# Queuing the conversions of the expert weights behind named pieces of the work under way

## The chip, the cores and the metric

One core of one Trainium2 chip runs the program. The metric is the device time of one execution in microseconds (us); a time shown for a kernel is the median of several executions. The engines are TensorE (PE, with its weight loads as PEld), VectorE (DVE), ScalarE (ACT), GpSimd (POOL) and SyncE (SP, which issues most of the DMAs). Each engine works through its own queue in order: an instruction that waits holds up everything behind it on that engine.

## The reference

Three stages follow each other; the change touches the last one and its seam with the second.

```python
attn_out = _attn_ref(q, k, v, omega)            # linear attention with random features, 4 x 8 heads x 576 x 64
x = attn_out.transpose(0, 2, 1, 3).reshape(2304, 512)
h = x @ w_in                                    # dense: 512 -> 2048
x = np.maximum(0.01 * h, h) @ w_out             # 2048 -> 512
logits = x @ w_gate                             # experts: 8, 512 -> 1024 -> 512
e_idx = np.argmax(logits, axis=1)
...
for e in range(8):
    mask = e_idx == e
    h = np.maximum(x[mask] @ w1[e], 0.0)
    out[mask] = gate_w[mask, None] * eom[mask, e, None] * (h @ w2[e])
```

## The kernel before

Every float32 product is made from two rounded parts: an operand is split into a high and a low part (`hi_lo`: ACT or DVE copies the rounded value, then DVE subtracts it from the source), and TensorE multiplies high by high, high by low and low by high. So each weight has to be converted before it can be used.

**Dense stage.** The 2304 rows go in 9 chunks c of 256 rows, the 2048 inner features in 8 units u. `h_unit(c, u)` is 24 matmuls (L463 to L465) into `hp`, followed on ACT by the copy `g` (L468) and on DVE by the leaky maximum (L469), `gh` and `gl`. `x_unit(c, u)` is 12 matmuls (L482 to L484) that read `gh` and `gl`. The loop issues `h_unit` of the next pair, then `x_unit` of the present one, so TensorE works one unit ahead. The attention of later rows and the routing of finished chunks are woven in by `tick`; the routing ends in two scatters of 4-byte row numbers into the table `tab_d` (L594).

**Expert stage.** The rows of one expert are worked through in slots of 576 rows, NSLOT + 1 = 4 of them in the written-out part (s = 0 to 3). A slot is two blocks (256 rows, then 320 rows). A block first runs `hidden(f)` for f = 0 to 7: 12 matmuls each (L713 to L715) into one of two PSUM banks of `ps_a`, then on ACT the relu `ehh` (L716) and on DVE `ehl` (L717), which free the bank. Then `back(j)` runs for 2 or 3 row tiles: 24 matmuls each (L730 to L732), an eviction `eyr` and a scatter of rows to the output. Before the first two `back` of a block, `xt` transposes the rows of the block that follows and splits them into `exh` and `exl`.

**Weights of an expert.** A slot has 8 weight pieces of 512 KB. `Slot.weight(k)` does all of it in one call: it takes one of two raw buffers `eraw` (tag `wraw`), issues the load on SP (L668 or L670), takes two tiles of a ring of 32, and converts: `ewh` on ACT (L209), `ewl` on DVE (L212). The first slot's pieces are called after the units of the last dense chunk (c = 8, piece u after unit u). The pieces of the slot after the present one are called in both blocks of the present slot after `hidden(f)` for f = 4 to 7, with the number `4 * half + f - 4`.

A list scheduler orders the instructions of each engine ahead of time: by program position, with the instructions that are ready in its own model taken first, so that an instruction called late may be queued early. `high_priority` moves the `g`, `gh`, `gl` of `h_unit` forward. `tc.issue_after(ins)` adds an edge that only fixes order in a queue: what is traced inside it on the engine of `ins` is queued behind `ins`.

Of the kernel before, what the change touches and what calls it, by code (L numbers as in the profile page):

```python
# [16 lines left out]
ALU = mybir.AluOpType  # L17
# [65 lines left out]
def f32(ap):  # L83
    return ap.bitcast(F32)
# [3 lines left out]
def tile_kernel(ctx: ExitStack, tc: tile.TileContext, kT, k_nat, v_nat, qT, q_nat, om, w_in, w_out, wg, w1, w2, out, stop=None, dbg=None):  # L88
# [46 lines left out]
    with ExitStack() as pa:  # L135
# [71 lines left out]
        def hi_lo(dst_hi, dst_lo, src, hi_eng, lo_eng):  # L207
            if hi_eng is nc.scalar:
                nc.scalar.copy(dst_hi, src)  # L209
            else:  # L210
                hi_eng.tensor_copy(dst_hi, src)
            lo_eng.tensor_sub(dst_lo, src, f32(dst_hi))  # L212


        order = [(k, u, h) for u in range(NU) for k in ("in", "out") for h in range(2)]
# [4 lines left out]
        groups = {}  # L220
        both_done = [False]
        newest = []
        kvs = {}
        xdone, hdone = {}, {}
        xT = {}
# [228 lines left out]
        def h_unit(c, u):  # L454
            assert xdone.get(c) == CH * NH // 2, (c, u, xdone)
            hdone[c] = u + 1
            xh, xl = xT[c]
            hp = ps_h.tile([P, 2, CH], F32, name="hp", tag="h")
            wh, wl = win[u]
            for i in range(2):  # L460
                for d in range(ND):
                    a, b_ = wh[:, d, i * P:(i + 1) * P], wl[:, d, i * P:(i + 1) * P]
                    nc.tensor.matmul(hp[:, i, :], a, xh[:, d, :], start=d == 0, stop=False)  # L463
                    nc.tensor.matmul(hp[:, i, :], a, xl[:, d, :], start=False, stop=False)  # L464
                    nc.tensor.matmul(hp[:, i, :], b_, xh[:, d, :], start=False, stop=d == ND - 1)  # L465
            with tc.high_priority(offset=AHEAD):
                g = sb.tile([P, 2, CH], F32, name="g", tag="g", bufs=1)
                nc.scalar.copy(g, hp)  # L468
                nc.vector.scalar_tensor_tensor(g, hp, 0.01, g, op0=ALU.mult, op1=ALU.max)  # L469
                gh = sb.tile([P, 2, CH], F32R, name="gh", tag="gh")  # L470
                gl = sb.tile([P, 2, CH], F32R, name="gl", tag="gl")
                hi_lo(gh, gl, g, nc.vector if c > 1 else nc.scalar, nc.vector)
            return gh, gl

        def x_unit(c, u, gg, acc):
# [173 lines left out]
        class Slot:  # L649


            def __init__(self, num, exp, at, first=False):
                self.c = nc.values_load(num[0:1, ds(at, 1)], engines=[SP], min_val=0, max_val=NC - 1)
                self.e = nc.values_load(exp[0:1, ds(at, 1)], engines=[SP], min_val=0, max_val=NE - 1)
                self.first = first
                self.w = []
                pool = rt if first else eb
                self.idx = pool.tile([P, 5], I32, name="idx", tag="idx", bufs=1 if first else 3)
                whole = tabv[ds(self.c, 1), 0:4 * P].rearrange("o (p i) -> (o p) i", i=4)
                rest = tabv[ds(self.c, 1), 4 * P:SLOT].rearrange("o (p i) -> (o p) i", i=1)  # L660
                for dst, src in ((self.idx[:, 0:4], whole), (self.idx[0:SLOT - 4 * P, 4:5], rest)):
                    got = nc.sync.dma_start(dst, src)
                    behind(got.ins, [o for k, o in placed if k == placed[-1][0]], "the table whole")

            def weight(self, k):
                raw = wst.tile([P, 1024], F32, name="eraw", tag="wraw")
                if k < 4:
                    nc.sync.dma_start(raw, w1v[ds(self.e, 1), k].rearrange("o p f -> (o p) f"))  # L668
                else:
                    nc.sync.dma_start(raw.rearrange("p (i n) -> p i n", i=2), w2v[ds(self.e, 1), k - 4].rearrange("o p i n -> (o p) i n"))  # L670
                hi = wring.tile([P, 1024], F32R, name="ewh", tag="w")
                lo = wring.tile([P, 1024], F32R, name="ewl", tag="w")
                hi_lo(hi, lo, raw, nc.scalar, nc.vector)
                self.w.append((hi, lo))

        class Block:
            def __init__(self, slot, half):
# [27 lines left out]
            def hidden(self, f):  # L705
                if f == 0:
                    self.hh = eb.tile([P, EFF // P, PART], F32R, name="ehh", tag="ehh", bufs=1)
                    self.hl = eb.tile([P, EFF // P, PART], F32R, name="ehl", tag="ehl", bufs=1)
                n = self.n
                t = ps_a.tile([P, 512], F32, name="eht", tag="a")[:, 0:n]  # L710
                for d in range(ND):
                    wh, wl = (w[:, f * P:(f + 1) * P] for w in self.slot.w[d])
                    nc.tensor.matmul(t, wh, self.xh[:, d, 0:n], start=d == 0, stop=False)  # L713
                    nc.tensor.matmul(t, wh, self.xl[:, d, 0:n], start=False, stop=False)  # L714
                    nc.tensor.matmul(t, wl, self.xh[:, d, 0:n], start=False, stop=d == ND - 1)  # L715
                nc.scalar.activation(self.hh[:, f, 0:n], t, AF.Relu)  # L716
                nc.vector.scalar_tensor_tensor(self.hl[:, f, 0:n], t, 0.0, f32(self.hh[:, f, 0:n]), op0=ALU.max, op1=ALU.subtract)  # L717

            def back(self, j, apart=True, final=False):

# [43 lines left out]
        def early():  # L764

            full = counts(ends, "full")
            incl = rt.tile([P, NC], F32, name="incl0", tag="incl0")
            nc.vector.tensor_tensor_scan(incl, ones_f, full, 0.0, op0=ALU.mult, op1=ALU.add)
            nc.vector.scalar_tensor_tensor(picked, incl, 1.0, full, op0=ALU.is_equal, op1=ALU.mult)
            none = rt.tile([P, NC], F32, name="none", tag="none")  # L770
            at = rt.tile([P, 1], F32, name="at", tag="at")
            nc.vector.tensor_scalar(none, incl, 0.0, None, op0=ALU.is_equal, op1=ALU.add, accum_out=at)
            num = rt.tile([1, 1], I32, name="num0", tag="num0")
            nc.vector.tensor_scalar_min(num, at[0:1], NC - 1.0)
            return Slot(num, expert_of(num, 1, "exp0"), 0, first=True)
# [32 lines left out]
        for i, (c, u) in enumerate(pairs):  # L808
# [35 lines left out]
                    tick()  # L844
            if slot is None and c == NCH - 2 and not routes and not any(c_ < 0 for c_, _ in flow):
                slot = early()
            if c == NCH - 1:
                slot.weight(u)
                if u == NU - 2:
                    for d in range(ND):  # L850
                        block.xt(d)
# [21 lines left out]
    with ExitStack() as pb:  # L873
        eb = pb.enter_context(tc.tile_pool(name="eb", bufs=2, reuse_waits="tile"))
        late = [f for it in routes for f in it if f is not nop]
        for s in range(NSLOT + 1):
            for half in range(2):
                last = s == NSLOT and half == 1
                for f in range(EFF // P):
                    block.hidden(f)  # L880
                    if late:
                        late.pop(0)()
                        if not late:
                            num, exp, nsl = listed()
                    if f == 3 and half == 0 and s < NSLOT:
                        other = Slot(num, exp, s)
                    if f >= 4 and s < NSLOT:
                        other.weight(4 * half + f - 4)
                    if f == 3 and not last:
                        following = second if s == half == 0 else Block(slot, 1) if half == 0 else Block(other, 0)  # L890
                        if following is not second:
                            following.rows()
                for j in range(len(block.tiles)):
                    if not last and j < 2:
                        following.xt(2 * j)
                        following.xt(2 * j + 1)
                    block.back(j, final=last)
                block = None if last else following
            slot = other if s < NSLOT else None

        n_slots = nc.values_load(nsl[0:1, 0:1], min_val=NSLOT, max_val=NSLOT + NE)  # L901
        with tc.For_i(NSLOT, n_slots) as s:
            one = Slot(num, exp, s)
            for k in range(8):
                one.weight(k)
            for half in range(2):
                b_ = Block(one, half)
                b_.rows()
                for d in range(ND):
                    b_.xt(d)  # L910
                for f in range(EFF // P):
                    b_.hidden(f)
                for j in range(len(b_.tiles)):
                    b_.back(j, False)
# [69 lines left out]
```

## Time and profile before

| | |
|---|---|
| median of 3 runs | 886.59 us (882.37 to 889.65) |
| profiled execution, its own time | 887.9 us |
| its span, first to last instruction | 886.2 us |
| mean granted TensorE clock | 0.981 of 2.4 GHz |
| busy: PE / PEld / DVE / ACT / POOL | 840.5 / 734.0 / 449.8 / 307.0 / 179.5 us |
| bytes moved by DMA | 73.55 MB, mean 83 GB/s |

The profiled execution is 1.7 us longer than its span. Busy time of TensorE counts overlapping matmuls once. An idle stretch carries the instruction that ended it ("<-"), found from semaphore events.

### The profile page before, as it was taken

How to read it: one execution, taken by the hardware profiler on the slowest of the kernel's cores; microseconds unless marked ns; L12 is line 12 of the kernel's file. 1: busy time of each engine (PE TensorE's matmuls, PEld its weight loads, DVE VectorE, ACT ScalarE, POOL GpSimd, SP SyncE). 2: the span in 40 equal slices, each digit the busy share in tenths (PEclk: the TensorE clock that was granted, in tenths of full speed). 3: DMA queues.
4: the chain of work that ended last, by engine and by line, in shares of the span. 5: the costliest groups of instructions: out<-in, count | busy, mean ns of one | idle time of the engine just before them, and what ended most of it. 6: DMA issues, size and time to landing. Idle time of an engine off the chain costs nothing. (4 is left out here: it accounts for less than half of the span.)

```text
span 886.2 us, 13999 instructions
## 1 busy us (share of the span) xinstructions
PE 840.5 (95%) x5299; PEld 734.0 (83%) x5299; DVE 449.8 (51%) x1142; ACT 307.0 (35%) x755; POOL 179.5 (20%) x253
## 2 busy tenths in 40 slices
PE   9889998999999999999999999997996999999996
PEld 7768777798899899988889899876886779888894
DVE  6899879626545445445554444454335433512220
ACT  4666655424324224323322232142125432411210
POOL 3545544301221012122010010120013211220001
PEclk9899999999999999999999999999999999999998
DMA  7636554301542021152020000155026622410001
GB/s 225 209 116 192 189 179 138 123 1 31 74 108 78 2 43 53 35 97 60 19 43 6 1 25 1 36 186 72 1 94 208 204 80 98 150 54 21 10 24 33
DMA packets 46153, 73.55 MB, mean 83 GB/s; under 512 B 6017, under 2 KB 28673, under 8 KB 46082
## 3 DMA queue, kind: packets, MB, share of 16 engines
q1 hardware_dynamic: 42562, 63.14, 25.7%
q0 software_dynamic: 3520, 9.47, 3.4%
q8 instruction: 44, 0.72, 0.4%
q14 instruction: 27, 0.22, 0.1%
HBM read 62.00 MB, written 10.59 MB: 82 GB/s over the span
## 5 line engine op out<-in xcount | busy, mean ns | idle before, releaser
L463 PE MATMUL hp<-xh,wih 128*128 128x256 f32 x576 | 167.2, 290 | 2.3 <-DVE xl L212 2.0
L464 PE MATMUL hp<-xl,wih 128*128 128x256 f32 x576 | 162.7, 282 | 0.1
L465 PE MATMUL hp<-xh,wil 128*128 128x256 f32 x576 | 162.1, 281 | 0.0
L482 PE MATMUL acc<-woh,gh 128*128 128x512 f32 x288 | 123.8, 430 | 1.4 <-ACT kv L373 1.4
L484 PE MATMUL acc<-woh,gl 128*128 128x512 f32 x288 | 116.6, 406 | 6.8 <-DVE gl L212 6.8
L319 ACT ACTIVATE h<-pw,bias 128x128 f32<-128x128 f32 x288 | 84.8, 372 | 107.5 <-DVE bias L311 87.7
L469 DVE SCALAR_TENSOR_TENSOR g<-hp,g 128x512 f32<-128x512 f32 x72 | 49.6, 689 | 130.7 <-ACT g L468 118.8
L483 PE MATMUL acc<-wol,gh 128*128 128x512 f32 x288 | 114.8, 399 | 0.0
L463 PEld LDWEIGHTS hp<-xh,wih 128*128 128x128 f32 x576 | 109.7, 190 | 5.5 <-issue 2.4
L464 PEld LDWEIGHTS hp<-xl,wih 128*128 128x128 f32 x576 | 109.6, 190 | 2.2 <-DVE xl L212 0.3
L465 PEld LDWEIGHTS hp<-xh,wil 128*128 128x128 f32 x576 | 109.5, 190 | 0.0
L468 ACT COPY g<-hp 128x512 f32<-128x512 f32 x72 | 42.2, 586 | 134.2 <-PE hp L465 129.6
L713 PE MATMUL eht<-exh,ewh 128*128 128x256 f32 (+1 forms) x256 | 76.9, 301 | 8.9 <-DVE ehl L717 7.2
L714 PE MATMUL eht<-exl,ewh 128*128 128x256 f32 (+1 forms) x256 | 76.4, 298 | 0.4 <-DVE exl L212 0.4
L715 PE MATMUL eht<-exh,ewl 128*128 128x256 f32 (+1 forms) x256 | 76.0, 297 | 0.0
L290 PE MATMUL pw<-om_raw,xpair 128*128 128x256 f32 (+1 forms) x260 | 72.0, 393 | 2.3 <-ACT h L319 2.3
L270 POOL TENSOR_TENSOR nat<-nat 128x256 f32<-128x256 f32 (+1 forms) x65 | 44.8, 692 | 136.8 <-DMA nat<-k_nat 59.0
L484 PEld LDWEIGHTS acc<-woh,gl 128*128 128x128 f32 x288 | 54.9, 191 | 20.5 <-DVE gl L212 8.4
L212 DVE TENSOR_TENSOR ewl<-eraw,ewh 128x1024 fp32r<-128x1024 f32 x32 | 39.1, 1225 | 59.9 <-ACT ewh L209 49.8
L482 PEld LDWEIGHTS acc<-woh,gh 128*128 128x128 f32 x288 | 54.6, 190 | 12.9 <-ACT kv L373 1.8
L730 PE MATMUL eyt<-ewh,ehh 128*128 128x512 f32 (+1 forms) x160 | 64.3, 402 | 0.6 <-ACT ehh L716 0.6
L731 PE MATMUL eyt<-ewl,ehh 128*128 128x512 f32 (+1 forms) x160 | 63.4, 396 | 0.0
(157 smaller groups left out, 1470.9 us busy)
## 6 DMA issues: line engine op xcount, KB each, us to landing
eraw<-w SPq DMA_DIRECT2D x32, 512.0 KB, 4.0
wraw<-w_in SPq DMA_DIRECT2D x16, 512.0 KB, 6.1
wraw<-w_out SPq DMA_DIRECT2D x16, 512.0 KB, 3.4
x_d<-rows SPq DMA_DIRECT2D x9, 514.0 KB
xpair<-qT SPq DMA_DIRECT2D x18, 256.0 KB, 9.0
nat<-q_nat SPq DMA_DIRECT2D x30, 128.0 KB, 2.6
nat<-k_nat SPq DMA_DIRECT2D x27, 128.0 KB, 2.6
xpair<-kT SPq DMA_DIRECT2D x12, 256.0 KB, 3.4
```

Of the source, the lines that this page charges most:

```text
L290: nc.tensor.matmul(pj[:, 2 * j:2 * j + k // HD, :], st["raw"][0:k, j * P:(j + 1) * P], om_raw[0:k, 0:M * k // HD], start=True, stop=True)
L319: nc.scalar.activation(h[:, j, :], src[:, j // 2, j % 2], AF.Exp, bias=bias[:, j:j + 1], scale=sc)
L463: nc.tensor.matmul(hp[:, i, :], a, xh[:, d, :], start=d == 0, stop=False)
L464: nc.tensor.matmul(hp[:, i, :], a, xl[:, d, :], start=False, stop=False)
L465: nc.tensor.matmul(hp[:, i, :], b_, xh[:, d, :], start=False, stop=d == ND - 1)
L482: nc.tensor.matmul(acc[t], a, h_, start=u == 0 and i == 0, stop=False)
L483: nc.tensor.matmul(acc[t], a, l_, start=False, stop=False)
L484: nc.tensor.matmul(acc[t], b_, h_, start=False, stop=u == NU - 1 and i == 1)
L713: nc.tensor.matmul(t, wh, self.xh[:, d, 0:n], start=d == 0, stop=False)
L714: nc.tensor.matmul(t, wh, self.xl[:, d, 0:n], start=False, stop=False)
L715: nc.tensor.matmul(t, wl, self.xh[:, d, 0:n], start=False, stop=d == ND - 1)
L730: nc.tensor.matmul(t, a, wh, start=f == 0, stop=False)
```

## The change

`weight(k)` is cut into `fetch(k)`, the load into a raw buffer, and `split(k)`, the two ring tiles and the conversion; `split(k)` then calls `fetch(k + 2)`. Conversions are traced under `issue_after`, so that each is queued behind a given instruction on ACT and another on DVE: in the last dense chunk behind the copy `g` on ACT and the subtraction `gl` on DVE of the unit issued last, in the expert stage behind the relu and the `ehl` of the `hidden(f)` issued last. The two first loads are called when the slot is known. In the expert stage the turns are given in two lists, as pairs of half and place (a number f is after `hidden(f)`, "bj" after `back(j)`): during s = 0 the first seven are in the second block and the eighth is in the first block of s = 1; during s = 1 and 2 four are in each block. Loads, conversions and matmuls are the same in number and size.

```diff
-            lo_eng.tensor_sub(dst_lo, src, f32(dst_hi))
+            return lo_eng.tensor_sub(dst_lo, src, f32(dst_hi)).ins
...
-                nc.scalar.copy(g, hp)
+                last_g[:] = [nc.scalar.copy(g, hp).ins]
...
-                hi_lo(gh, gl, g, nc.vector if c > 1 else nc.scalar, nc.vector)
+                last_g.append(hi_lo(gh, gl, g, nc.vector if c > 1 else nc.scalar, nc.vector))
...
-            def weight(self, k):
+            def fetch(self, k):
                 raw = wst.tile([P, 1024], F32, name="eraw", tag="wraw")
...
+                self.raw.append(raw)
+
+            def split(self, k, after=()):
+
                 hi = wring.tile([P, 1024], F32R, name="ewh", tag="w")
                 lo = wring.tile([P, 1024], F32R, name="ewl", tag="w")
-                hi_lo(hi, lo, raw, nc.scalar, nc.vector)
+                with ExitStack() as order_:
+                    for ins in after:
+                        order_.enter_context(tc.issue_after(ins))
+                    hi_lo(hi, lo, self.raw[k], nc.scalar, nc.vector)
                 self.w.append((hi, lo))
+                if k + 2 < 8:
+                    self.fetch(k + 2)
...
                 slot = early()
+                slot.fetch(0)
+                slot.fetch(1)
             if c == NCH - 1:
-                slot.weight(u)
+                slot.split(u, last_g)
...
+        turns_late = [(1, 1), (1, 3), (1, 5), (1, 7), (1, "b0"), (1, "b1"), (1, "b2"), None]
+        turns_even = [(0, 5), (0, 7), (0, "b0"), (0, "b1"), (1, 1), (1, 3), (1, 5), (1, 7)]
+        behind_ = None
+
+        def weights_at(s, half, x):
+            if s < NSLOT:
+                for k, at in enumerate(turns_late if s == 0 else turns_even):
+                    if at == (half, x):
+                        other.split(k, behind_)
+            if s == 1 and (half, x) == (0, 1):
+                slot.split(7, behind_)
...
-                    block.hidden(f)
+                    behind_ = block.hidden(f)
...
                     if f == 3 and half == 0 and s < NSLOT:
                         other = Slot(num, exp, s)
-                    if f >= 4 and s < NSLOT:
-                        other.weight(4 * half + f - 4)
+                        other.fetch(0)
+                        other.fetch(1)
+                    weights_at(s, half, f)
...
                     block.back(j, final=last)
+                    weights_at(s, half, f"b{j}")
```

`hidden` returns its relu and its `ehl` instruction. The loop for slots beyond the four written out is changed in the same way, without `issue_after`.

## Rows read from the trace of the kernel before

**Rows 1.** The page's head and its slices: busy tenths, granted clock.

```profile
span 886.2 us, 13999 instructions
PE 840.5 (95%) x5299; PEld 734.0 (83%) x5299; DVE 449.8 (51%) x1142; ACT 307.0 (35%) x755; POOL 179.5 (20%) x253
...
PE   9889998999999999999999999997996999999996
```

**Rows 2.** TensorE's waits, 560 to 887 us: us in total, times, longest.

```profile
PE eht L713 <- DVE ehl L717: 7.2, 3, 5.6
PE acc L484 <- DVE gl L212: 6.8, 2, 6.2
PE eht L713 <- ACT exh L209: 1.5, 2, 0.9
PE eyt L730 <- ACT ehh L716: 0.6, 1, 0.6
PE eht L714 <- DVE exl L212: 0.4, 1, 0.4
```

**Rows 3.** ACT in order of time, 606 to 620 us: start, us, instruction.

```profile
607.16 0.59 ACT L468 COPY g<-hp 128x512 f32<-128x512 f32 x1 [2.46 <-DVE gl L212]
615.70 1.05 ACT L209 CAST ewh<-eraw 128x1024 fp32r<-128x1024 f32 x1 [7.95 <-DMA eraw<-w]
618.69 0.59 ACT L468 COPY g<-hp 128x512 f32<-128x512 f32 x1 [1.95 <-DVE gl L212]
```

**Rows 4.** DVE in order of time, same stretch.

```profile
608.51 0.43 DVE L211 CAST gh<-g 128x512 fp32r<-128x512 f32 x1
616.78 1.23 DVE L212 TENSOR_TENSOR ewl<-eraw,ewh 128x1024 fp32r<-128x1024 f32 x1 [7.84 <-ACT ewh L209]
617.92 0.68 DVE L212 TENSOR_TENSOR gl<-g,gh 128x512 fp32r<-128x512 f32 x1
```

**Rows 5.** SP and POOL in order of time: the last load of slot 0, a scatter.

```profile
604.40 0.38 SPq L670 DMA_DIRECT2D eraw<-w  x1
602.64 0.98 POOL L594 DMA_INDIRECT tab_d<-tokid,r_pi  x1 [0.30 <-issue]
```

**Rows 6.** ACT in order of time, 650 to 677 us.

```profile
663.30 1.05 ACT L209 CAST ewh<-eraw 128x1024 fp32r<-128x1024 f32 x1 [10.60 <-DMA eraw<-w]
...
666.09 0.75 ACT L209 CAST exh<-ext 128x320 fp32r<-128x320 f32 x2
...
672.96 1.04 ACT L209 CAST ewh<-eraw 128x1024 fp32r<-128x1024 f32 x1 [2.72 <-DMA eraw<-w]
673.91 0.43 ACT L716 ACTIVATE ehh<-eht 128x320 fp32r<-128x320 f32 x1
```

**Rows 7.** DVE in order of time, same stretch.

```profile
674.04 1.22 DVE L212 TENSOR_TENSOR ewl<-eraw,ewh 128x1024 fp32r<-128x1024 f32 x1 [1.88 <-ACT ewh L209]
675.18 0.48 DVE L717 SCALAR_TENSOR_TENSOR ehl<-eht,ehh 128x320 fp32r<-128x320 f32 x1
```

**Rows 8.** Stretches: us, busy by engine (instructions), then granted clock, DMA share, GB/s.

```profile
612.44:618.66 6.22, 0.00 (x1) 0.00 (x1) 1.83 (x2) 1.05 (x1) 0.00 (x0) 0.89 0.17 49
618.66:623.10 4.44, 4.44 (x11) 3.48 (x12) 1.81 (x3) 0.59 (x1) 0.00 (x0) 0.50 0.01 4
623.10:626.37 3.27, 3.27 (x25) 3.27 (x24) 0.00 (x0) 0.00 (x0) 0.00 (x0) 0.85 0.00 0
626.37:629.17 2.80, 2.80 (x14) 2.25 (x13) 1.81 (x3) 0.59 (x1) 0.00 (x0) 1.00 0.00 0
...
626.37:632.00 5.63, 5.63 (x38) 5.07 (x37) 1.81 (x3) 0.59 (x1) 0.00 (x0) 1.00 0.00 0
...
675.72:678.92 3.20, 3.20 (x13) 3.19 (x14) 1.47 (x2) 1.38 (x2) 0.18 (x1) 0.53 0.68 200
...
733.55:747.80 14.25, 14.25 (x99) 14.23 (x98) 4.52 (x9) 4.36 (x9) 1.62 (x4) 1.00 0.16 45
```

**Rows 9.** The raw weight tile: its loads and its conversions over the whole span.

```profile
L209 ACT CAST ewh<-eraw x32: 1041/1051/1068, 577.4 to 769.2; 128x1024 fp32r<-128x1024 f32 x32
L212 DVE TENSOR_TENSOR ewl<-eraw,ewh x32: 1215/1226/1228, 578.5 to 770.3; 128x1024 fp32r<-128x1024 f32 x32
...
DMA to landing us min/median/max: 3.6/4.0/5.8
```

**Rows 10.** SP in order of time: the load that the conversion at 672.96 used.

```profile
666.90 0.33 SPq L668 DMA_DIRECT2D eraw<-w  x1
```

**Rows 11.** ACT and DVE around one conversion of slot 3.

```profile
746.07 0.44 ACT L716 ACTIVATE ehh<-eht 128x320 fp32r<-128x320 f32 x1 [1.32 <-PE eht L715]
746.40 1.99 ACT L209 CAST ewh<-eraw 128x1024 fp32r<-128x1024 f32 x2
```

More of the change, by code (lines that the diff above doesn't have):

```diff
@@ L222, in tile_kernel @@
         newest = []
+        last_g = []
         kvs = {}
@@ L655, in __init__ @@
                 self.first = first
-                self.w = []
+                self.w, self.raw = [], []
                 pool = rt if first else eb
@@ L715, in hidden @@
                     nc.tensor.matmul(t, wl, self.xh[:, d, 0:n], start=False, stop=d == ND - 1)
-                nc.scalar.activation(self.hh[:, f, 0:n], t, AF.Relu)
-                nc.vector.scalar_tensor_tensor(self.hl[:, f, 0:n], t, 0.0, f32(self.hh[:, f, 0:n]), op0=ALU.max, op1=ALU.subtract)
+                a = nc.scalar.activation(self.hh[:, f, 0:n], t, AF.Relu)
+                b_ = nc.vector.scalar_tensor_tensor(self.hl[:, f, 0:n], t, 0.0, f32(self.hh[:, f, 0:n]), op0=ALU.max, op1=ALU.subtract)
+                return a.ins, b_.ins
             def back(self, j, apart=True, final=False):
@@ L903, in tile_kernel @@
             one = Slot(num, exp, s)
+            one.fetch(0)
+            one.fetch(1)
             for k in range(8):
-                one.weight(k)
+                one.split(k)
             for half in range(2):
```

## The prediction, made before the result was known

> **What bounds the kernel now.** The page's head says it first: TensorE is busy for 840.5 of 886.2 us [rows 1], DVE for about half of it and the rest for less. A change that moves no matmul can therefore only win what TensorE loses: its idle time, and the stretches in which it runs at the lower clock. The slices show where to look: but for the last slice the only ones under 8 are the 7 in slice 28 and the 6 in slice 31 of 22 us each, at some 610 and 675 us [rows 1]. That is the seam from the dense stage to the experts and the first expert slot, the place of the edit. I then asked for TensorE's waits from 560 us to the end: 7.2 + 6.8 + 1.5 + 0.6 + 0.4 = 16.5 us, and the list is complete [rows 2]. The releasers are DVE's `ehl` and `gl`, ACT's `exh` and `ehh` and DVE's `exl`: short splits and evictions, none of them a matmul or a load. The question is what made them late, and that is read in the two queues.
>
> **Seam.** TensorE waits 6.22 us for `gl` in x_unit [rows 2, 8]. DVE had finished `gh` at 608.9 and was then idle for 7.84 us, because the next instruction in its queue was an `ewl`; `gl`, which was ready to run, stood behind it and ran at 617.92 [rows 4]. The `ewl` waited for ACT's `ewh`, which itself waited 7.95 us for its load until 615.70 [rows 3]. The load had been issued at 604.40, right behind a scatter of the routing, and took 11.3 us [rows 3, 5], against a usual 3.6 to 5.8 [rows 9]. So one late load, of a piece that only the first `back` needs, stopped the dense stage through a queue.
>
> **First expert slot.** ACT was idle for 10.60 us before 663.30 with a conversion at its head, and `exh` of the next block ran only at 666.09; the relu of the first hidden unit ran at 673.91 behind a conversion that had waited 2.72 us for its load [rows 6], and its `ehl` at 675.18 behind an `ewl` [rows 7]. This made the 5.6 us wait for a bank. The same happens on a smaller scale when the next slot begins: the rest of the `ehl` wait and the `ehh` wait, 7.2 - 5.6 + 0.6 = 2.2 us [rows 2].
>
> **The clock.** The long idle stretch is followed by one at 0.50, 1.2 of 2.4 GHz, the lower of the two levels [rows 8]. The x_unit there needs 4.44 us for 10 matmuls; at full clock 12 take 2.80 us, so 10 take 2.33, and 2.1 us are lost. The 24 matmuls behind it take 3.27 us at a mean of 0.85; an undisturbed pair of x_unit and h_unit takes 5.63, less 2.80 that is 2.83 for the h_unit: another 0.4. After the bank wait 12 matmuls take 3.20 us at 0.53; a full-clock block of 96 takes 14.25, so 12 take 1.78, and 1.4 are lost [rows 8]. Sum 3.9 us.
>
> **The change, part by part.**
>
> *Dense conversions.* Piece u moves from wherever its model thought it ready to a place behind `g` of unit u + 1 on ACT and behind `gl` of the same unit on DVE. What stood in front of `gl` in the seam can't stand there now: gain 6.8 us of waits and 2.1 + 0.4 of clock, 9.3. Behind a conversion that waits for its load there is now the next unit's `g`, 5.6 us later, and `gl` is needed only after a further x_unit and h_unit. ACT then has 0.59 + 1.05 and DVE 1.81 + 1.23 us of work in 5.6 us [rows 3, 8, 9]. A load is issued when the conversion two before it is done, two units or 11 us ahead; even the 11.3 us load of the seam would be late by less than the 3 us that the order leaves. Cost 0. Pieces 6 and 7 both come behind the last unit, at about 623 to 628 us on the shortened time axis, and are first needed by `back`, one block of hidden units (some 13 us) later.
>
> *Loads.* Same 512 KB, same two raw buffers, same SP queue; a load still cannot start before the DVE half of the conversion two before it. The calls pass the index loads and the store of routed rows in SP's queue; SP waits there for DVE and for scatters, but the loads' own condition comes later than either in the shortened order. Cost 0; if a load is pushed behind such a store, it loses some us of a lead of 11.
>
> *Expert conversions.* They leave the head of the queue before `exh` and relu. Gain: the whole `ehl`, `exh`, `ehh` and `exl` waits, 9.7 us, and 1.4 of clock. The raw buffers of slot 1 are filled before the turn (1, 1), as they were filled before 664 us now.
>
> *The new wait.* Behind a conversion at (1, f) stands the relu of f + 1. Take the start of a 320-row relu as zero. The conversion starts at 0.33 [rows 11], ACT is done at 1.38, and `ewl` ends at 2.6 (1.23 from rows 9). `ehl` of f + 1 is done at 3.0, and TensorE wants its bank for f + 3 after two units of 1.78, at 3.5. So 0.5 us is to spare if the data are there. The load for the conversion four units on is issued at 2.65 and wanted at 4 x 1.76 + 0.33 = 7.4: 4.75 us, or 5.25 with what is to spare. The median load of 4.0 fits. The longest that ended a wait here took from 666.90 to 672.96, 6.1 us [rows 6, 10], and would cost 0.8. Conversions 2 and 3 of slot 1 and 6 and 7 of slots 2 and 3 stand in such places: 6 turns, from 0 to 6 x 0.8 = 5 us. I take 1.0, since the median is what most loads take. Turns at f = 5 and 7 of a first block, and those among the `back`, find their data there or have no hidden unit behind them. The turn (0, 1) of s = 1 stands in shorter units and may cost 0.2, inside the same 1.0.
>
> **Sum.** 16.5 + 3.9 - 1.0 = 19.4 us less. From the profiled 887.9 (its span of 886.2 and 1.7 around it, which the change doesn't touch) that gives 868.5; that run is 1.3 above the median of the runs, so from 886.6 it gives 867.2. What is late next is nothing in this stage: TensorE then works without a break to the end of the last block, where a tail of output scatters stays.
>
> **Weighing a page.** The trace shows the bank wait ended by an `ehl` that had stood behind an `ewl` [rows 7], while a whole block of 96 matmuls runs through the same two banks without idle time where no conversion comes between [rows 8]. The Trainium skill, Perfetto Trace Analysis, section Identifying Performance Opportunities, says that a gap which keeps repeating can mean too few buffers of SBUF or PSUM for the next tile. By that rule the two banks would be at fault and the waits for `ehl` would stay; the block without idle time speaks against it, so it gets a small chance below.
>
> **Rivals.**
> 1. *Two banks of `ps_a` are too few* for units of this length, whatever stands in DVE's queue: the seam is mended, the expert stage is not. Of the 20.4 us, 7.2 + 0.6 of waits and 1.4 of clock stay: 866 + 9 = 875. Chance 0.03.
> 2. *The order doesn't hold where it matters.* The edge fixes only what a conversion stands behind, not what stands behind it, nor that its load has landed. The conversions at "b0" to "b2" hang on f = 7 alone, so they may still block ACT up to the next block's relu, for the 2.2 us seen now at each of three slot changes, 6.6 us; or one of the two large stalls (seam 9.3, first slot 9) stays in another place. 873 to 878, say 876. Chance 0.15. For it: the order comes from a model that already placed loads too early. Against: in the `back` stretches now, ACT waits for loads and TensorE doesn't.
> 3. *No effect:* another wait of the same size takes their place, for instance the first expert rows or the routing table: 885 to 888. Against: neither ended any wait of TensorE [rows 2]. Chance 0.05.
> 4. *Slower.* Spread into the hidden units, the loads are late at all 6 tight turns. This decides from a load time of 5.25 us; the loss is 6 x (L - 5.25). With the load of 11.3 us that met a scatter it is 36 us, less 20.4 won: 902. To come out slower by 1% at all, L must be above 10. No load beside gathers and output scatters came near that. Chance 0.05.
>
> **How the numbers follow.** Forecast 867, chance 0.72. Its own range is 862 (the whole 20.4 gives 866, and the shown runs lie up to 4 us under their median) to 872 (5 us of late loads). To hold 8 in 10 with the rivals, most of the second has to be covered: 862 to 879. One per cent, about 9 us, is what a measurement here tells from no change: faster by more than that means below 877.7, which takes the forecast, the first rival and two thirds of the second: 0.85. Within: the rest of the second and the third, 0.10. Slower: 0.05.
>
> **What would show it.** Right: no idle time of TensorE before L484 for `gl`; no stretch at 0.50 between 610 and 680 us; `ewh` directly behind a `g` or a relu; the block of second-half hidden units of s = 0 takes about 14.2 us instead of 24; waits of TensorE from 560 us on of 1 to 3 us in all. Wrong: waits of L713 for `ehl` that recur every second hidden unit (rival 4), or ACT idle with a conversion at its head when a block begins (rival 2). The number would also be wrong if the new order of queues delays the routing or the row gathers, which cause no wait now.

## The result

| | before | after |
|---|---|---|
| median | 885.58 us (6 runs, 882.37 to 889.65) | 864.00 us (6 runs, 862.06 to 867.23) |
| ratio, 95% interval | | 0.976 (0.9735 to 0.9785) |
| profiled execution, its span | 887.9, 886.2 us | 862.73, 861.0 us |
| mean granted TensorE clock | 0.981 | 0.989 |

The kernel became faster by 2.4%, 21 us (19 to 23.5). The forecast was 867, with 862 to 879 as its range.

**The profile after.** The page's head and two of its rows of slices, to be laid beside [rows 1]:

```profile
span 861.0 us, 13985 instructions
PE 831.8 (97%) x5299; PEld 729.0 (85%) x5299; DVE 450.7 (52%) x1142; ACT 306.5 (36%) x755; POOL 176.1 (20%) x253
...
PE   9889988999999999999999999999999999999996
...
PEclk9899999899999999999999999999999999999998
```

The 7 and the 6 of slices 28 and 31 are gone; the matmuls are the same 5299. The list of TensorE's waits from 560 us to the end, five lines in [rows 2], holds only its header now: no wait at all. The stretches that were at 0.50 or had an idle TensorE [rows 8] read like this (columns as there):

```profile
660.00:680.00 20.00, 20.00 (x107) 16.73 (x106) 11.13 (x15) 8.57 (x15) 2.02 (x4) 1.00 0.61 186
651.49:665.74 14.25, 14.25 (x99) 14.24 (x98) 6.96 (x10) 5.89 (x10) 5.95 (x8) 1.00 0.50 157
...
600.00:620.00 20.00, 20.00 (x128) 17.91 (x127) 11.96 (x19) 6.14 (x8) 0.00 (x0) 1.00 0.62 106
```

TensorE is busy in all of the two stretches of 20 us, where in the kernel before it was busy for 13.14 (660 to 680) and 13.78 us (600 to 620) of them. The line between them is the second block of hidden units of s = 0: 14.25 us, the time of an undisturbed block [rows 8], at full clock.

**The seam, after.** ACT and then DVE in order of time, against [rows 3, 4]:

```profile
606.73 0.59 ACT L469 COPY g<-hp 128x512 f32<-128x512 f32 x1 [4.09 <-PE hp L466]
611.52 1.05 ACT L209 CAST ewh<-eraw 128x1024 fp32r<-128x1024 f32 x1 [4.20 <-DMA eraw<-w]
612.47 0.58 ACT L469 COPY g<-hp 128x512 f32<-128x512 f32 x1
612.95 1.05 ACT L209 CAST ewh<-eraw 128x1024 fp32r<-128x1024 f32 x1
```

```profile
612.60 1.23 DVE L212 TENSOR_TENSOR ewl<-eraw,ewh 128x1024 fp32r<-128x1024 f32 x1 [3.37 <-ACT ewh L209]
613.74 0.69 DVE L470 SCALAR_TENSOR_TENSOR g<-hp,g 128x512 f32<-128x512 f32 x1
614.46 0.43 DVE L211 CAST gh<-g 128x512 fp32r<-128x512 f32 x1
614.92 0.69 DVE L212 TENSOR_TENSOR gl<-g,gh 128x512 fp32r<-128x512 f32 x1
615.53 1.22 DVE L212 TENSOR_TENSOR ewl<-eraw,ewh 128x1024 fp32r<-128x1024 f32 x1
```

The late load is still there. Piece 4 was issued at 601.94 and is converted at 611.52, 9.6 us later; ACT stands still for 4.20 us at the head of its queue, as it did for 7.95 before. What differs is who is behind it: the `g` of the next unit, whose last matmul ended at about 612.3. It loses 0.1 us, `gl` is ready at 615.6, and the x_unit that reads it begins at 617.79, straight behind the h_unit.

**The first expert slot, after.** ACT, against [rows 6]:

```profile
662.25 0.44 ACT L726 ACTIVATE ehh<-eht 128x320 fp32r<-128x320 f32 x1 [1.09 <-PE eht L725]
663.67 1.05 ACT L209 CAST ewh<-eraw 128x1024 fp32r<-128x1024 f32 x1 [0.98 <-DMA eraw<-w]
664.63 0.43 ACT L726 ACTIVATE ehh<-eht 128x320 fp32r<-128x320 f32 x1
665.77 0.44 ACT L726 ACTIVATE ehh<-eht 128x320 fp32r<-128x320 f32 x1 [0.72 <-PE eht L725]
666.11 1.04 ACT L209 CAST ewh<-eraw 128x1024 fp32r<-128x1024 f32 x1
```

These are f = 5, a conversion that waited for its load, then f = 6 and f = 7. Of the 6 turns that the prediction called tight it is the only one whose load was late.

**What ACT waits for.** The view of the raw tile lists, for before and then after, the idle time in front of the conversions `ewh` that a load ended (us, times):

```profile
...
  DMA eraw<-w: 47.0, 16
...
```

```profile
...
  DMA eraw<-w: 15.6, 8
...
```

So the change did not do away with ACT waiting for loads. It left a third of that, in places where TensorE does not notice.

**Where the profiled difference lies.** The two profiled executions are 25.2 us apart. By the start of the last dense chunk (an h_unit that starts at 563.17 before, 561.31 after) 1.9 us of this are there already, while the queues of all engines hold the same instructions in the same order up to there (only two DVE records at 227 us, 0.03 us apart, stand the other way round): run to run, not the change. Over the twelve kernels shown here one and the same matmul ahead of the change starts anywhere from 550.7 to 555.8 us. From the start of that chunk to the end of the last matmul the two differ by 23.3.

### The profile page after: what moved, and what is told of

Same layout as the page of the kernel before. It is cut to its first block, busy times and chain, and to the rows that moved or that the text cites. A ratio compares the mean times of both kernels' runs of the same rounds, so it can differ in the third digit from the quotient of the medians.

```text
span 861.0 us, 13985 instructions
## 1 busy us (share of the span) xinstructions
PE 831.8 (97%) x5299; PEld 729.0 (85%) x5299; DVE 450.7 (52%) x1142; ACT 306.5 (36%) x755; POOL 176.1 (20%) x253
## 5 line engine op out<-in xcount | busy, mean ns | idle before, releaser
L727 DVE SCALAR_TENSOR_TENSOR ehl<-eht,ehh 128x256 fp32r<-128x256 f32 (+1 forms) x64 | 29.1, 456 | 67.2 <-ACT ehh L726 64.3
```

## The experiments

Each kernel differs from the kernel after or before by the lines shown; line numbers shift by a few between kernels. `weight` is again one call that loads and converts, as in the kernel before. A ratio is to the kernel before, timed in turn on the same chip.

### The two parts alone

**seam_only**: the dense part of the change, the expert calls of before.

```diff
-                        other.fetch(0)
-                        other.fetch(1)
-                    weights_at(s, half, f)
+                    if f >= 4 and s < NSLOT:
+                        other.weight(4 * half + f - 4)
...
-                    weights_at(s, half, f"b{j}")
```

> Only the last dense chunk is changed (first slot: loads ahead, conversions queued behind g and gl); the expert stage calls its weights as before. If the order in the queues of ACT and DVE is the cause, the wait for gl, the two small waits before it and the low clock behind it go, about 10.5 us: 875 us, and the waits for ehl and exh of the first expert slot stay at about 9 us. If instead the gain of the whole comes from the expert stage alone (spread), this run stays within 3 us of the kernel before.

Measured: 873.1 against 883.45 us, ratio 0.9903 (0.9873 to 0.9934), by the ratio 8.6 us less (5.8 to 11.2). TensorE's waits from 560 us:

```profile
PE eht L727 <- DVE ehl L731: 5.5, 4, 3.1
PE eht L727 <- ACT exh L209: 1.2, 1, 1.2
...
```

**experts_only**: the dense calls of before, the expert part of the change.

```diff
                 slot = early()
-                slot.fetch(0)
-                slot.fetch(1)
...
-                slot.split(u, last_g)
+                slot.weight(u)
```

> Only the expert stage is changed; the last dense chunk calls its weights as before. Order in the queues as the cause: the waits for exh, exl, ehl and ehh and the low clock behind them go, about 11 us: 874 to 875 us, and the 6.2 us wait for gl in the seam stays. With the run before this one the two parts should add up to the whole gain of 21.6. If one stall only moves (what is saved in the seam is lost at the first slot), the two gains don't add up.

Measured: 871.28 us, 0.9877 (0.9821 to 0.9934), 10.9 us less (5.8 to 15.8). TensorE's waits:

```profile
PE acc L485 <- DVE gl L212: 5.9, 2, 5.3
PE eht L727 <- ACT exh L209: 0.6, 1, 0.6
```

Each part takes away the waits of its own stage and leaves those of the other. 0.9903 x 0.9877 = 0.978, close to the 0.976 of the whole: the two gains add up and neither needs the other.

### Is it the edge, the place of the call, or the early load?

**no_edges**: everything of the change but the order.

```diff
-                    for ins in after:
+                    for ins in ():
```

> The whole change with all its new places and early loads, but without issue_after: the conversions may be queued anywhere. Order as the cause: nothing is left of the gain, 883 to 888 us, with the wait for gl of about 6 us back. Rival, the loads ahead or the spreading of the conversions over both parts of a block are what helps: 864 to 870 us.

Measured: 883.64 us, 1.0003 (0.9972 to 1.0035). The waits are back:

```profile
PE eht L723 <- DVE ehl L727: 7.3, 4, 3.0
PE acc L485 <- DVE gl L212: 5.6, 2, 5.0
PE eht L723 <- ACT exh L209: 1.6, 2, 1.0
...
```

Loads called two ahead and calls moved to other places bring nothing measurable by themselves (0.3% either way), because the scheduler puts the instructions back into almost the order of before: from 560 us on, the two traces differ only around 680 us, in the place of one conversion, one relu with its `ehl`, and a few matmuls of a `back`. The other way round, a kernel with the edges, but with each load called right before its conversion, has the instructions of the kernel after in the same order on all five engines; it was not run for that reason. A load is held by its raw buffer, not by the place of its call.

**last_piece**: the kernel before with one edge, for the last piece of slot 0.

```diff
-                slot.split(u, last_g)
+                slot.weight(u, last_g if u == 7 else ())
```

> The kernel before, with issue_after for one conversion only: piece 7 of the first slot behind g and gl of the last dense unit. Order as the cause: that one conversion made the 6.2 us wait for gl and the low clock behind it, 6.4 + 2.5, so 876 to 877 us. Rival, the late load itself (11.3 us) is what costs, whoever stands behind it: the wait goes to another piece or to the first expert block, and the time stays at 883 to 887 us.

Measured: 875.35 us, 0.9914 (0.9886 to 0.9943), 7.6 us less (5.0 to 10.1); the `gl` wait is down from 6.8 [rows 2] to

```profile
...
PE acc L485 <- DVE gl L212: 0.6, 1, 0.6
...
```

From 560 us on, its trace has the instructions of the kernel before in the same order on every engine, but for that one conversion on ACT and its other half on DVE. So nearly all that the dense part wins hangs on the place of one conversion pair, the one that [rows 3, 4] show.

### What the places in the expert stage are worth

**old_turns**: the edges, but the conversions behind f = 4 to 7 of both halves, as they are called before.

```diff
-                    weights_at(s, half, f)
+                    if f >= 4 and s < NSLOT:
+                        other.split(4 * half + f - 4, behind_)
...
-                    weights_at(s, half, f"b{j}")
```

> The edges of the change, but the pieces called in the old places: four in each block, after hidden units 4 to 7, queued behind that unit's relu and ehl. If order alone matters, about the time of the changed kernel, 0.976 to 0.980 of the kernel before: two conversions with their data there stand behind units 5 and 6, the rest falls into the backs. If spreading them over both parts of a block matters, the conversions crowd against relu and ehl: 0.983 or more, with waits of TensorE for ehl or ehh at the end of the hidden units.

Measured: 868.97 against 881.2 us, 0.9849 (0.9815 to 0.9882). ACT when slot 0 goes over to its second block:

```profile
650.04 1.05 ACT L209 CAST ewh<-eraw 128x1024 fp32r<-128x1024 f32 x1 [9.65 <-DMA eraw<-w]
652.64 1.05 ACT L209 CAST ewh<-eraw 128x1024 fp32r<-128x1024 f32 x1 [1.55 <-DMA eraw<-w]
653.59 0.68 ACT L751 ACTIVATE eyr<-eyt,esc 128x512 f32<-128x512 f32 x1
654.17 0.75 ACT L209 CAST exh<-ext 128x320 fp32r<-128x320 f32 x2
```

The first conversion stands where the edge put it, behind a hidden unit of the first block, but SP reads the next slot's table only at 644.92 and issues the first load at 646.21, so the data are there at 650. Behind it stands `exh`, and TensorE waits for that (1.3 us) and for an `ehl` (3.2). An edge to a point at which the data cannot be there makes the stall it was to prevent.

**late_first**: the new places for the slot after the first alone, the old ones with edges for the rest (`weights_at` at s = 0 and for the last piece at s = 1; `split(4 * half + f - 4, behind_)` from s = 1 on). **after_again**: the kernel after, timed beside it.

> The changed kernel, but only the slot after the first keeps its new turns (all in the second block, the last one in the next slot); the two later slots are called in the old places (units 4 to 7 of both blocks), with the edges. If the places matter only where the loads can't be there yet (the routing table of the next slot), this run equals the changed kernel run beside it within 1.5 us and has no wait of the hidden units. If spreading over both parts matters in every slot, it is slower by 2 us or more, with waits for ehl or ehh in the second and third slot.

> The changed kernel itself, for comparison on the same chip: 0.974 to 0.979 of the kernel before, no wait of TensorE behind 560 us.

Measured: 863.11 us, 0.977 (0.9748 to 0.9791), and 862.4 us, 0.9752 (0.9733 to 0.9771), against 883.19; in both TensorE waits for nothing behind 560 us. Spreading over both parts of a block is thus worth nothing measurable for the slots whose table is long there; holding the first slot's pieces back to its second block is worth about 5 us, by old_turns against turns_0246 (below, same chip), which keeps them back too.

### How tight the turns are

**turns_0246**: the turns among the hidden units one unit earlier. **turns_each**: one piece behind every hidden unit of the second block.

```diff
-        turns_late = [(1, 1), (1, 3), (1, 5), (1, 7), (1, "b0"), (1, "b1"), (1, "b2"), None]
-        turns_even = [(0, 5), (0, 7), (0, "b0"), (0, "b1"), (1, 1), (1, 3), (1, 5), (1, 7)]
+        turns_late = [(1, 0), (1, 2), (1, 4), (1, 6), (1, "b0"), (1, "b1"), (1, "b2"), None]
+        turns_even = [(0, 4), (0, 6), (0, "b0"), (0, "b1"), (1, 0), (1, 2), (1, 4), (1, 6)]
```

```diff
+        turns_late = [(1, 0), (1, 1), (1, 2), (1, 3), (1, 4), (1, 5), (1, 6), None]
+        turns_even = [(1, 0), (1, 1), (1, 2), (1, 3), (1, 4), (1, 5), (1, 6), (1, 7)]
```

> The changed kernel with all turns one hidden unit earlier (0, 2, 4, 6 in place of 1, 3, 5, 7), so that the conversion that waits for a load stands before a unit that needs a bank. By the same sum: nothing where the load takes 4 us, and 0.3 to 1 us of a wait for ehl where it takes more than 5.25, so 0 to 2 us over the changed kernel, 0.976 to 0.978. Rival, no turn is tight: no wait at all.

> The changed kernel with the pieces called after every hidden unit of the second block instead of every second one. By the sum for a conversion that stands between two relus (0.5 us to spare, a load wanted 4.75 us after its issue): the third and fourth conversion come 1 us late in front of units that still need a bank, 0.5 to 1.5 us of waits for ehl in each of three slots, 2 to 4 us in all: 0.978 to 0.982. If loads and conversions have room enough anyway: no wait, 0.976. If the load is what bounds: more than 1 us for every conversion, 0.99.

Measured: 863.87 us, 0.9797 (0.9764 to 0.9831), and 867.96 us, 0.9844 (0.9813 to 0.9875), against 881.2. The one wait of TensorE in turns_0246, and ACT there:

```profile
PE eht L723 <- DVE ehl L727: 1.0, 1, 1.0
```

```profile
660.36 0.44 ACT L726 ACTIVATE ehh<-eht 128x320 fp32r<-128x320 f32 x1 [1.32 <-PE eht L725]
662.13 1.05 ACT L209 CAST ewh<-eraw 128x1024 fp32r<-128x1024 f32 x1 [1.33 <-DMA eraw<-w]
663.08 0.43 ACT L726 ACTIVATE ehh<-eht 128x320 fp32r<-128x320 f32 x1
663.88 0.44 ACT L726 ACTIVATE ehh<-eht 128x320 fp32r<-128x320 f32 x1 [0.37 <-PE eht L725]
```

The conversion behind f = 4 should have started at 660.36 + 0.33 = 660.69 and is 1.44 us late. With the 0.5 us that the prediction found to spare, TensorE should lose 0.9; it loses 1.0. In turns_each two conversions stand behind neighbouring units and the third finds no data; ACT:

```profile
655.84 1.04 ACT L209 CAST ewh<-eraw 128x1024 fp32r<-128x1024 f32 x1
657.27 0.44 ACT L726 ACTIVATE ehh<-eht 128x320 fp32r<-128x320 f32 x1 [0.38 <-PE eht L725]
659.03 0.44 ACT L726 ACTIVATE ehh<-eht 128x320 fp32r<-128x320 f32 x1 [1.32 <-PE eht L725]
662.33 1.04 ACT L209 CAST ewh<-eraw 128x1024 fp32r<-128x1024 f32 x1 [2.86 <-DMA eraw<-w]
```

TensorE waits 3.9 us in four places (the longest 2.5), and the time is 4.1 us above that of turns_0246. The waits are of the size that was expected; both ratios came out a little above their expected ranges, which still touch the intervals. The mechanism of rival 4 is real; it needs a denser row of turns than the change has.

### Order or banks?

**before_4banks**: the kernel before, with every second pair of hidden units in two further PSUM banks (not in the first block, when these are taken).

```diff
-                t = ps_a.tile([P, 512], F32, name="eht", tag="a")[:, 0:n]
+                more = f % 4 > 1 and not (self.slot.first and self.n == CH)
+                t = (ps_h if more else ps_a).tile([P, 512], F32, name="eht", tag="h" if more else "a")[:, 0:n]
```

> The kernel before with four PSUM banks for the hidden units in place of two (all blocks but the first). If the order of the queues is the cause, two more units of 1.76 us can run while the evictions stand behind a conversion: the 5.6 us wait shrinks to about 2 and the smaller ones go, 5 to 7 us less in all, and the seam's 6.2 stays: 0.992 to 0.994. If two banks are too few as such, all waits of the hidden units go, 9 to 11 us: 0.988 or less. If neither, 1.00.

Measured: 880.44 against 881.2 us, 0.9974 (0.9954 to 0.9994), 2.3 us less (0.5 to 4.1). TensorE's waits for `eht`, and then ACT and DVE in the first slot:

```profile
...
PE eht L714 <- DVE ehl L718: 5.4, 2, 2.7
PE eht L714 <- ACT exh L209: 2.1, 2, 1.4
...
```

```profile
666.57 1.05 ACT L209 CAST ewh<-eraw 128x1024 fp32r<-128x1024 f32 x1 [1.52 <-DMA eraw<-w]
667.52 0.43 ACT L717 ACTIVATE ehh<-eht 128x320 fp32r<-128x320 f32 x1
671.32 1.04 ACT L209 CAST ewh<-eraw 128x1024 fp32r<-128x1024 f32 x1 [3.36 <-DMA eraw<-w]
672.27 0.76 ACT L717 ACTIVATE ehh<-eht 128x320 fp32r<-128x320 f32 x2
674.39 1.05 ACT L209 CAST ewh<-eraw 128x1024 fp32r<-128x1024 f32 x1 [1.36 <-DMA eraw<-w]
```

```profile
672.39 1.23 DVE L212 TENSOR_TENSOR ewl<-eraw,ewh 128x1024 fp32r<-128x1024 f32 x1 [3.12 <-ACT ewh L209]
673.54 0.88 DVE L718 SCALAR_TENSOR_TENSOR ehl<-eht,ehh 128x320 fp32r<-128x320 f32 x2
```

My own expectation of 5 to 7 us missed as well. I had taken the late conversion for a single event that two more banks would bridge. The rows show a queue that advances at the pace of its loads for several conversions in a row, with one or two relus after each; four banks fill up behind it as two did, only later.

## Why the prediction was right

**The seam, 9.3.** Right in mechanism and in size: 8.6 (5.8 to 11.2) alone, 7.6 with one edge. One step under it was wrong. I gave a load in this stage a lead of two units, 11 us. Piece 4 was issued at 601.94 and its turn came at 607.3, behind the `g` of 606.73: 5.4 us. The two units took 8.5 us (`g` at 598.27, 601.10 and 606.73), since the dense units, with other work woven between them, are not evenly spaced; and the conversion that frees the raw buffer takes another 3.2 of the lead (598.76 to 601.91), which I had not taken off. The load was late by 4.2 us, not by "less than the 3 us that the order leaves". It cost nothing because the order left more than that: the `g` behind it was due only at about 612.35 and `gl` only at 617.8. The room was not large: an estimate from these rows is that with the 11.3 us load of the kernel before, `gl` would have been ready at 617.3.

**The expert part, 9.7 + 1.4.** Right: 10.9 (5.8 to 15.8) measured alone. One of its terms belongs to the seam: an `exh` wait of 0.65 us ends at 595.83, in the last dense chunk, and experts_only keeps it (0.6 above).

**The new wait, 1.0 with bounds 0 to 5.** The working of one turn was right: a conversion 1.44 us late in turns_0246 cost 1.0, as the 0.5 us to spare says. The places were wrong. A relu held up at f + 1 delays the bank of unit f + 3, and all six turns I counted stand at f = 5 and 7, behind which the block has no unit f + 3. In the kernel after the one late turn is there, 663.67 where 662.25 + 0.33 = 662.58 was due, 1.1 us, and it cost nothing. At f = 1 and 3, where it would have cost, no conversion waited for its load in any slot. The term is 0, and the "6 x (L - 5.25)" of rival 4 doesn't hold for the turns that it was made for. The load times under it were read too narrowly as well: the 3.6, 4.0 and 5.8 us of [rows 9] are of the four loads, of 32, whose landing that trace has, and the longest load that ended a wait of ACT in the expert stage of the kernel before took 6.5 us (700.00 to 706.46), not 6.1.

**What the sum left out.** The waits and the clock made 20.4. I summed, for both profiled kernels, by how much each start of a matmul behind 560 us follows the one before it by more than the usual distance behind a matmul of that size (0.2325 us for 512 columns, 0.1175 for 256, 0.1467 for 320): 25.4 us before, 2.9 after, a difference of 22.5. The `ehh` wait of 0.6 us is not in it, since it follows a transpose of 64 columns; of the 20.4, 19.8 are. The other 2.7 us are the pauses' own. From start to start the idle stretch of 6.22 us [rows 8] takes 6.39, because the profile counts idle time only from the end of the matmul before it, 0.39 us after its start; the other pauses show the same 0.16. The first matmul behind a pause then takes 0.1 us more than its neighbours (0.17 at the lower clock). Nine pauses (the ninth, of 0.12 us, is too short for the list) at 0.27 make 2.4, nearly all of the missing term. The start behind the transpose comes after 0.88 us where 0.20 is usual, another 0.7, the `ehh` wait among it. With these, and with 0 for the new wait, 23.2 of the 23.3 us are placed, where I forecast 19.4; the measured 19 to 23.5 holds both.

**The rivals.** *Two banks too few* fell: in the kernel after the same two banks cause no wait at all, and in the one before two more bring 2.3 us where the rule would have brought 9. The Trainium skill's rule on repeating gaps (Perfetto Trace Analysis, Identifying Performance Opportunities) names a possible cause; here the gap repeated with the loads, not with the buffers. *The order doesn't hold where it matters:* ACT does stand idle at "b0" and "b2" of s = 0 with a conversion at its head, for 2.38 and 2.06 us (up to 670.08 and 676.11). But the eviction behind the first still had to wait 0.75 us for TensorE, and behind the second nothing was due before an eviction at 683.57. *No effect* fell by the result; its one true part is no_edges, by which the early loads and the moved calls are worth nothing. *Slower by late loads* showed itself only where I made the turns denser.

**What was not tried.** Doubling every load in the kernel after, which would have given the load time from which it becomes slower, and four banks in the kernel after, where no wait is left to remove.

## What to carry to other kernels

When TensorE waits for a short operation of another engine, look at what stood ahead of that operation in its engine's queue; a conversion that waits for a load should stand behind the work whose result is due soonest, and its own wait can then stay. Fix such an order only to points at which the data can be there: an edge to a place ahead of the next slot's table cost about 5 us. Before moving calls about, compare the queues that come out, since a scheduler may undo the move, and one edge may do nearly all of it.

## What the runs showed of the hardware

The first 512 KB load issued behind the two scatters of the routing near 600 us took 8.0 to 11.3 us in each of the twelve kernels, whether it was piece 4 or piece 7. The other loads whose time the traces give took 3.3 to 7.9 us, with medians of 3.6 to 4.2 us by kernel. DMA activity of the kernel after from 595 to 615 us, in 40 slices of 0.5 us, as busy tenths and GB/s, then what POOL and SP issued there:

```profile
DMA  5992599200000000900083403999247997000005
GB/s 164 369 393 90 226 391 387 51 0 1 0 0 0 0 0 4 127 0 0 0 53 37 25 33 33 86 156 33 41 143 254 406 410 254 37 0 0 0 0 45
```

```profile
596.81 1.01 POOL L595 DMA_INDIRECT tab_d<-tokid,r_pi  x1 [15.06 <-DVE r_pi L592]
598.13 0.98 POOL L595 DMA_INDIRECT tab_d<-tokid,r_pi  x1 [0.30 <-issue]
```

```profile
...
601.94 0.39 SPq L671 DMA_DIRECT2D eraw<-w  x1
```

The load is issued at 601.94 and the next one at 604.86. But for one slice the DMA engines move next to nothing up to 605; up to 609.5 they move 25 to 156 GB/s, though in some slices they are busy for nine tenths; most of the two loads goes over between 609.5 and 612, at 143 to 410 GB/s. In the kernel before it is the last load, with 11.3 us [rows 3, 5]. The scatters of 4-byte row numbers just ahead are the obvious suspects, but no run took them away, so the cause stays open.
